# A first DFT step with d on the partitions, and two DMA transposes inside SBUF in place of an exchange through DRAM

## The chip, the cores and the metric

One core of one Trainium2 chip. The metric is the device time of one launch in microseconds; runs of one kernel mostly agree within 0.3%. A single core has no second die to compare with; every run used here is of the state "fast", within 1.5% of the fastest of its kernel. TensorE (PE) does the matrix multiplications and leaves the results in PSUM; ScalarE (ACT) and VectorE (DVE) bring them to SBUF, the memory that the next step reads (an "evacuation"). GpSimd (POOL) issues the loads of x and, at the start, of some weights; SyncE (SP) issues all other transfers. Sixteen DMA engines serve both queues: q1 is what SP issues, q0 what POOL issues.

## The reference

A Fourier layer, then a feed-forward block on its rows. Cut to what matters:

```python
X = np.fft.rfft(x, axis=1)                 # x: (8, 3008, 256)
Yr = Xr @ w_r - Xi @ w_i + b_r             # mix over the 256 features, real part
Yi = Xr @ w_i + Xi @ w_r + b_i
# soft threshold by 0.01 on Yr and Yi
y = np.fft.irfft(Yr + 1j * Yi, n=3008, axis=1)
h = y.reshape(24064, 256) @ w_in           # w_in: (256, 2048)
out = (s * np.maximum(h, 0) ** 2 + b) @ w_out
```

The kernel splits 3008 = 94 x 32: a DFT over n1 (94) with 96 real outputs, then one over n2 (32) with twiddles, the mix and the threshold, and the same two steps back. Batch by batch, the four steps are woven between the matmuls of the feed-forward block of an earlier batch.

## The kernel before

The first step of batches 1 to 7. `A_t` is the 94x96 DFT matrix. It is the stationary operand, and x streams past it:

```python
xpool = ctx.enter_context(tc.tile_pool(name="xp", bufs=4))      # one batch of x is 4 tiles
upool = ctx.enter_context(tc.tile_pool(name="up", bufs=3))
uspool = ctx.enter_context(tc.tile_pool(name="usp", bufs=5))
# ...
def s1_units(b, more_banks=False):
    ud = dpool.tile([96, N2, D], F16, name="ud", tag="ud")       # in DRAM
    hold = {}
    def unit(i):                                                 # 16 units
        c, j = divmod(2 * i, XCH)
        if j == 0:
            hold["u"] = upool.tile([P, XCH, D], F16, name="u", tag="u")
        ps = other_bank() if more_banks and i % 2 else one_bank()
        nc.tensor.matmul(ps[0:96, :], A_t[0:N1, :],
                         x16[(b, c)][0:N1, j * D : (j + 2) * D], start=True, stop=True)
        u = hold["u"]
        evac(u[0:96, j : j + 2, :], ps[0:96, :].rearrange("p (j d) -> p j d", j=2), 512)
        if j == XCH - 2:
            nc.sync.dma_start(out=ud[:, c * XCH : (c + 1) * XCH, :], in_=u[0:96])
        if i == N2 // 2 - 1:                                     # back, 128 rows (k, n) a tile
            uv = ud.rearrange("k n d -> (k n) d").rearrange("(q p) d -> p q d", p=P)
            for q in range(4):
                t = uspool.tile([P, 6, D], F16, name="us", tag="us")
                nc.sync.dma_start(out=t, in_=uv[:, 6 * q : 6 * q + 6, :])
                us[(b, q)] = t
```

The second step uses `us` as its stationary operand (`psf<-F_t,us` in the profile). The x loads and the schedule:

```python
def emit_load_x(b, first=None):            # first: a tile to wait for, used for batch 2 only
    for c in range(4):
        t = xpool.tile([P, XCH * D], F16, name="x16", tag="x16")
        if first is not None:
            gate = nc.gpsimd.tensor_copy(out=t[0:1, 0:1], in_=first)
        nc.gpsimd.dma_start(...)            # 94 rows of 4096 bytes, cast from f32
# ...
for b in range(2, B):
    s0, s1, s2 = mark[b - 2], mark[b - 1], mark[b]      # slots of the feed-forward block
    schedule(s0 + 40, s1 - s0 - 48, s1_units(b))
    schedule(s1 + 2, s2 - s1 - 30, s23_units(b))
    schedule(s2 - 14, 12, s4_units(b))
    if b + 1 < B:
        plan.setdefault(s1 + 6, []).append(lambda b=b: emit_load_x(b + 1))
```

A load of x for batch b+1 can start when the x tile of batch b in the same buffer has been read for the last time. What decides that is the order in which the first step reads its four x tiles.

## Time and profile before

| | before |
|---|---|
| time, median of 4 runs | 852.05 us |
| TensorE busy, of the span of 849.4 us | 835.0 us |
| one unit of the first step on TensorE (one matmul of 94x512) | 0.22 us |
| first-step exchange, per batch | 4 writes and 4 reads of 384 KB |
| end of the last evacuation of u to the first second-step matmul | 9.4 to 12.2 us |

TensorE is the bound and hardly ever waits; the exchange is hidden in that last row's window. The prediction shows the lines that say so. One more, of the page's DMA part:

```profile
HBM read 52.54 MB, written 46.66 MB: 117 GB/s over the span
```

### The profile page before, as it was taken

The page shows a single profiled execution, that of the slowest core. Times are in us where ns is not written, and L with a number is a line of the kernel's source. Part 1 is how long each engine was busy: PE and PEld are TensorE (multiplying, and loading weights), DVE is VectorE, ACT ScalarE, POOL GpSimd, SP SyncE. Part 2 cuts the span into 40 slices and gives each one's busy share as a digit, 9 for nine tenths or more (in the row PEclk, how much of TensorE's full clock was granted, in tenths as well). Part 3 has the DMA queues.
Part 4 walks back from the last instruction along what each step waited for, and adds up shares of the span by engine and source line. Part 5 has one row for each costly group of instructions (what it writes and reads, how often), then busy time and mean ns, then how long its engine had stood idle before and what let it go on. Part 6 is the DMA issues. An engine that isn't in the chain of part 4 may idle for free.

```text
span 849.4 us, 17085 instructions
## 1 busy us (share of the span) xinstructions
PE 835.0 (98%) x6645; PEld 600.5 (71%) x6645; DVE 697.0 (82%) x1027; ACT 643.2 (76%) x856; POOL 46.6 (5%) x72
## 2 busy tenths in 40 slices
PE   8899999999999999999999999999999999999997
PEld 7757777777677766777677776777667777766765
DVE  6898987888888987888878888888977888776674
ACT  5898887787778787787777887787877787766673
POOL 5321000000000000000000000000000000000000
PEclk9999999999999999999999999999999999999999
DMA  7937457324761367324662247613354223411111
GB/s 165 161 104 162 108 148 185 101 76 100 177 186 54 92 159 184 109 78 103 171 177 65 74 106 199 172 40 92 100 156 118 62 79 98 112 33 38 38 44 50
DMA packets 105458, 95.07 MB, mean 112 GB/s; under 512 B 9510, under 2 KB 97578, under 8 KB 104034
## 3 DMA queue, kind: packets, MB, share of 16 engines
q1 hardware_dynamic: 98930, 79.57, 32.6%
q0 software_dynamic: 6448, 14.42, 10.7%
q8 instruction: 52, 0.85, 0.4%
q14 instruction: 28, 0.23, 0.1%
HBM read 52.54 MB, written 46.66 MB: 117 GB/s over the span
## 4 chain that ended last, share of the span: by engine, by line
PE 88%; DVE 4%; ACT 3%; DMA 2%; issue 1%; POOL 0%; SPq 0%; DVEq 0%; ACTq 0%; POOLq 0%
PE psa L832 36%; PE psh L761 36%; PE psf L627 4%; PE psf L562 2%; PE psf L613 2%; PE psf L598 2%; PE psf L657 2%; PE psf L710 2%; ACT rt L768 1%; DVE gt L775 1%; DMA x<-in_x_dram 1%; DMA out_dram<-ost 1%; PE psh L410 1%; ACT yt L160 0%; ACT vs L160 0%
## 5 line engine op out<-in xcount | busy, mean ns | idle before, releaser
L768 ACT ACTIVATE rt<-psh 128x1024 f32<-128x1024 f32 (+2 forms) x384 | 387.1, 1009 | 119.1 <-PE psh L761 117.7
L775 DVE TENSOR_TENSOR gt<-rt 128x1024 f16<-128x1024 f32 (+2 forms) x321 | 384.0, 1199 | 98.1 <-ACT rt L768 97.4
L832 PE MATMUL psa<-w_out_t,gt 128*128 128x256 f16 (+1 forms) x3024 | 454.3, 272 | 0.1
L832 PEld LDWEIGHTS <-gt 128*128 128x128 f16 (+1 forms) x3024 | 300.9, 101 | 187.2 <-issue 1.7
L761 PE MATMUL psh<-yt,w_in 128*128 128x512 f16 (+1 forms) x1344 | 396.7, 378 | 0.3 <-ACT rt L768 0.3
L761 PEld LDWEIGHTS <-w_in 128*128 128x128 f16 x1536 | 142.9, 98 | 27.4 <-issue 2.1
L842 DVE SCALAR_TENSOR_TENSOR ost<-psa,s_bc,bias_bc 128x512 f32<-128x512 f32 (+2 forms) x97 | 71.0, 732 | 8.3 <-PE psa L832 7.1
L772 ACT ACTIVATE gt<-rt 128x1024 f16<-128x1024 f32 (+2 forms) x63 | 66.2, 1050 | 1.0
L632 DVE TENSOR_TENSOR ring<-psf,s 128x512 f16<-128x512 f32 x84 | 57.5, 684 | 3.7 <-PE psf L627 2.9
L160 ACT CAST v<-psf 128x512 f16<-128x512 f32 x78 | 45.3, 582 | 18.7 <-PE psf L657 18.7
L160 ACT CAST xf<-psf 128x512 f16<-128x512 f32 x82 | 47.9, 585 | 10.9 <-PE psf L598 10.8
L160 ACT CAST u<-psf 96x512 f16<-96x512 f32 x77 | 44.5, 580 | 11.0 <-PE psf L562 10.7
L761 PE MATMUL psh<-tail,w_in 128*128 128x512 f16 (+1 forms) x192 | 52.1, 353 | 0.0
L627 PE MATMUL psf<-W_g,xf 128*128 128x256 f16 x336 | 50.4, 273 | 0.0
L160 ACT CAST yt<-psf 128x480 f16<-128x480 f32 (+2 forms) x75 | 38.1, 520 | 13.6 <-PE psf L710 13.6
L189 POOL DMA_DIRECT2D x<-in_x_dram x36 | 18.9, 530 | 429.3 <-PE psf L562 428.0
L562 PE MATMUL psf<-x,A_t 94*96 94x512 f16 x104 | 39.7, 381 | 1.7 <-ACT yt L160 0.5
L638 DVE TENSOR_TENSOR ring<-ring,high 128x512 f16<-128x512 f16 x84 | 35.5, 423 | 2.3
L639 DVE TENSOR_TENSOR ring<-ring 128x512 f16<-128x512 f16 x84 | 35.5, 422 | 1.9
L637 DVE TENSOR_TENSOR ring<-ring,low 128x512 f16<-128x512 f16 x84 | 35.4, 421 | 1.6
L627 PEld LDWEIGHTS <-xf 128*128 128x128 f16 x336 | 32.9, 98 | 3.8
L710 PE MATMUL psf<-C_t,vs 96*128 96x96 f16 x448 | 33.0, 205 | 0.1
(89 smaller groups left out, 501.9 us busy)
## 6 DMA issues: line engine op xcount, KB each, us to landing
out_dram<-ost SPq DMA_DIRECT2D x152, 128.0 KB
ud<-u SPq DMA_DIRECT2D x28, 384.0 KB
us<-ud SPq DMA_DIRECT2D x28, 384.0 KB
vd<-v SPq DMA_DIRECT2D x42, 256.0 KB
vs<-vd SPq DMA_DIRECT2D x14, 768.0 KB
x<-in_x_dram POOLq DMA_DIRECT2D x28, 376.0 KB, 5.9
ring<-ring SPq DMA_DIRECT2D x280, 32.0 KB
out_dram<-ost SPq DMA_DIRECT2D x16, 120.0 KB
```

The source lines that it names most:

```text
L160: return None, nc.scalar.copy(out=dst, in_=src)
L562: nc.tensor.matmul(ps[0:96, :], A_t[0:N1, :], x16[(b, c)][0:N1, j * D : (j + 2) * D], start=True, stop=True,)
L627: nc.tensor.matmul(ps[:, r, :], xt[:, 2 - r, dc], W_g[:, dc, r], start=(dc == 0), stop=(dc == DC - 1),)
L632: nc.vector.tensor_tensor(out=t, in0=ps, in1=hold[i // 2][:, i % 2].unsqueeze(1).to_broadcast([P, 2, D]), op=ALU.add,)
L638: nc.vector.tensor_tensor(out=m, in0=m, in1=high, op=ALU.min)
L710: nc.tensor.matmul(ps[:, j * 96 : (j + 1) * 96], vs[(b, h)][:, k, ec * P : (ec + 1) * P], C_t, start=True, stop=True,)
L761: nc.tensor.matmul(o, w_in_t[dc][:, mc * P : (mc + 1) * P], r, start=(dc == 0), stop=(dc == DC - 1),)
L768: nc.scalar.activation(out=rt[:, :, 0:w], in_=ps[:, :, 0:w], func=AF.Relu)
L772: nc.scalar.activation(out=gt[:, :, 0:w], in_=rt[:, :, 0:w], func=AF.Square)
L775: nc.vector.tensor_tensor(out=gt[:, :, 0:w], in0=rt[:, :, 0:w], in1=rt[:, :, 0:w], op=ALU.mult)
L832: nc.tensor.matmul(ps[0:size, h, :], gts[(ti, mc // 2)][:, mc % 2, sub * size : (sub + 1) * size], w_out_t[:, mc, :], start=(mc == 0), sto ...
L842: nc.vector.scalar_tensor_tensor(out=ost[0:size, 0:k], in0=ps[0:size, 0:k], scalar=s_bc[0:size], in1=bias_bc[0:size, 0:k], op0=ALU.mult, o ...
```

## The change

The intent: batches 1 to 7 take the form that batch 0 has already. x becomes the stationary operand and `A_t` streams, so the result has d on all 128 partitions. The second step needs (k, n) on the partitions, and two DMA transposes per batch bring it there without DRAM. The buffers are resized to make room (not shown: `vs` goes from two buffers of half the rows to one of all rows, and constants of batch 0 share a tile). The core of the diff:

```diff
-    upool = ctx.enter_context(tc.tile_pool(name="up", bufs=3))
-    uspool = ctx.enter_context(tc.tile_pool(name="usp", bufs=5))
+    upool = ctx.enter_context(tc.tile_pool(name="up", bufs=1))
+    uspool = ctx.enter_context(tc.tile_pool(name="usp", bufs=1))
...
         def unit(i):
-            c, j = divmod(2 * i, XCH)
-            if j == 0:
-                hold["u"] = upool.tile([P, XCH, D], F16, name="u", tag="u")
+            dc, g = divmod(i, N2 // 4)
+            if i == 0:
+                hold["u"] = upool.tile([P, DC, 96, N2], F16, name="u", tag="u")
+                us[b] = uspool.tile([P, NPAIR, D], F16, name="us", tag="us")
+            c, h = divmod(g, 2)
             ps = other_bank() if more_banks and i % 2 else one_bank()
-            nc.tensor.matmul(
-                ps[0:96, :], A_t[0:N1, :], x16[(b, c)][0:N1, j * D : (j + 2) * D],
-                start=True, stop=True,
-            )
+            for j in range(4):
+                lo = (4 * h + j) * D + dc * P
+                nc.tensor.matmul(
+                    ps[:, j * 96 : j * 96 + 96], x16[(b, c)][0:N1, lo : lo + P],
+                    A_t[0:N1, :], start=True, stop=True,
+                )
             u = hold["u"]
-            evac(u[0:96, j : j + 2, :], ps[0:96, :].rearrange("p (j d) -> p j d", j=2), 512)
-            if j == XCH - 2:
+            evac(
+                u[:, dc, :, 4 * g : 4 * g + 4],
+                ps[:, 0:384].rearrange("p (n k) -> p k n", k=96), 384,
+            )
+            if g == N2 // 4 - 1:
                 nc.sync.dma_start(
-                    out=ud[:, c * XCH : (c + 1) * XCH, :], in_=u[0:96]
+                    out=us[b][:, :, dc * P : (dc + 1) * P],
+                    in_=u[:, dc].rearrange("p k n -> p (k n)"),
+                    transpose=True,
                 )
-            if i == N2 // 2 - 1: ...            # the four reads from DRAM: gone
...
-        emit_load_x(2, us[(1, 3)][0:1, 0, 0:1])
+        emit_load_x(2, us[1][0:1, 0, 0:1])
```

`dc, g = divmod(i, N2 // 4)` walks through all four x tiles for the first half of d, then once more for the second half.

More of the change, by code (lines that the diff above doesn't have):

```diff
@@ L144 @@
     vpool = ctx.enter_context(tc.tile_pool(name="vp", bufs=3))
-    vspool = ctx.enter_context(tc.tile_pool(name="vsp", bufs=2))
+    vspool = ctx.enter_context(tc.tile_pool(name="vsp", bufs=1))
     ypool = ctx.enter_context(tc.tile_pool(name="yp", bufs=2))
@@ L220 @@
             nc.sync.dma_start(out=b_g[r : r + 1, i], in_=bv.unsqueeze(0))
-    F_c = uspool.tile([P, NPAIR, 2, N2], F16, name="F_c", tag="us")
+    first_c = uspool.tile([P, 4, NPAIR * 64], F16, name="first_c", tag="us")
+    F_c = first_c[:, 0].rearrange("p (q r k) -> p q r k", q=NPAIR, r=2)
+    T_c = first_c[:, 1].rearrange("p (q k) -> p q k", q=NPAIR)
+    F_2 = [first_c[:, 2 + i].rearrange("p (q k) -> p q k", q=H) for i in range(2)]
     b_h = cpool.tile([P, D], F16, name="b_h")
@@ L227 @@
     sel_t = cpool.tile([P, P], F16, name="sel_t")
-    T_c = uspool.tile([P, NPAIR, 64], F16, name="T_c", tag="us")
     eye_t = cpool.tile([P, P], F16, name="eye_t")
@@ L275 @@
     nc.vector.memset(T_t, 0.0)
-    F_2 = [uspool.tile([P, H, P], F16, name="F_2", tag="us") for _ in range(2)]
     for f in F_2:
@@ L466, in inv_dft @@
             )
-        for h in range(2):
-            vs[(0, h)] = vspool.tile([96, HW, D], F16, name="vs", tag="vs")
+        vs[0] = vspool.tile([P, N2, D], F16, name="vs", tag="vs")
         def turn(ec, k):
@@ L477, in turn @@
                 )
-            h, n = divmod(8 * k, HW)
             evac(
-                vs[(0, h)][:, n : n + 8, ec * P : (ec + 1) * P],
+                vs[0][0:96, 8 * k : 8 * k + 8, ec * P : (ec + 1) * P],
                 ps[0:96].rearrange("p h (j e) -> p (h j) e", e=P), 1024,
@@ L489, in last_dft @@
             for j in range(8):
-                h, k = divmod(n2 + j, HW)
                 nc.tensor.matmul(
                     ps[j // 4][:, (j % 4) * 96 : (j % 4) * 96 + 96],
-                    vs[(0, h)][:, k, ec * P : (ec + 1) * P], C_t,
+                    vs[0][0:96, n2 + j, ec * P : (ec + 1) * P], C_t,
                     start=True, stop=True,
@@ L552, in s1_units @@
     def s1_units(b, more_banks=False):
-        ud = dpool.tile([96, N2, D], F16, name="ud", tag="ud")
         hold = {}
         def unit(i):
-            c, j = divmod(2 * i, XCH)
-            if j == 0:
-                hold["u"] = upool.tile([P, XCH, D], F16, name="u", tag="u")
-            ps = other_bank() if more_banks and i % 2 else one_bank()
-            nc.tensor.matmul(
-                ps[0:96, :], A_t[0:N1, :], x16[(b, c)][0:N1, j * D : (j + 2) * D],
-                start=True, stop=True,
-            )
-            u = hold["u"]
-            evac(u[0:96, j : j + 2, :], ps[0:96, :].rearrange("p (j d) -> p j d", j=2), 512)
-            if j == XCH - 2:
+            dc, g = divmod(i, N2 // 4)
[3 more added lines that the diff above has]
+            c, h = divmod(g, 2)
+            ps = other_bank() if more_banks and i % 2 else one_bank()
+            for j in range(4):
[4 more added lines that the diff above has]
+                )
+            u = hold["u"]
+            evac(
+                u[:, dc, :, 4 * g : 4 * g + 4],
+                ps[:, 0:384].rearrange("p (n k) -> p k n", k=96), 384,
+            )
+            if g == N2 // 4 - 1:
                 nc.sync.dma_start(
-                    out=ud[:, c * XCH : (c + 1) * XCH, :], in_=u[0:96]
-                )
-            if i == N2 // 2 - 1:
-                uv = ud.rearrange("k n d -> (k n) d").rearrange("(q p) d -> p q d", p=P)
-                for q in range(4):
-                    t = uspool.tile([P, 6, D], F16, name="us", tag="us")
-                    nc.sync.dma_start(out=t, in_=uv[:, 6 * q : 6 * q + 6, :])
-                    us[(b, q)] = t
+                    out=us[b][:, :, dc * P : (dc + 1) * P],
+                    in_=u[:, dc].rearrange("p k n -> p (k n)"),
+                    transpose=True,
+                )
         return [lambda i=i: unit(i) for i in range(N2 // 2)]
@@ L593, in fwd_unit @@
             ps = bank.rearrange("p (r c j k) -> p r c j k", r=2, c=DC, j=2)
-            t = us[(b, i // 3)]
             for j in range(2):
-                q = (2 * i + j) % 6
                 for dc in range(DC):
                     nc.tensor.matmul(
-                        ps[:, :, dc, j, :], t[:, q, dc * P : (dc + 1) * P],
+                        ps[:, :, dc, j, :], us[b][:, 2 * i + j, dc * P : (dc + 1) * P],
                         F_t[:, 2 * i + j, :], start=True, stop=True,
@@ L670, in inv_unit @@
                 vv = vd.rearrange("q (k n) e -> (q k) (n e)", n=N2)
+                t = vs[b] = vspool.tile([P, N2, D], F16, name="vs", tag="vs")
                 for h in range(2):
-                    t = vspool.tile([96, HW, D], F16, name="vs", tag="vs")
                     nc.sync.dma_start(
-                        out=t.rearrange("k n e -> k (n e)"),
+                        out=t[0:96, h * HW : h * HW + HW].rearrange("k n e -> k (n e)"),
                         in_=vv[:, h * HW * D : (h + 1) * HW * D],
                     )
-                    vs[(b, h)] = t
         units = []
@@ L708, in unit @@
             for j in range(w):
-                h, k = divmod(n2 + j, HW)
                 nc.tensor.matmul(
                     ps[:, j * 96 : (j + 1) * 96],
-                    vs[(b, h)][:, k, ec * P : (ec + 1) * P], C_t,
+                    vs[b][0:96, n2 + j, ec * P : (ec + 1) * P], C_t,
                     start=True, stop=True,
```

## The prediction

> **What bounds the kernel now.** I read the page first (busy time and the forty slices), then the chain of waits, then the table of groups, then stretches of the timeline in order of time around the step that changes, for the tensor engine and for the SP queue.
>
> ```profile
> span 849.4 us, 17085 instructions
> PE 835.0 (98%) x6645; PEld 600.5 (71%) x6645; DVE 697.0 (82%) x1027; ACT 643.2 (76%) x856; POOL 46.6 (5%) x72
> PE   8899999999999999999999999999999999999997
> DMA  7937457324761367324662247613354223411111
> ...
> PE 88%; DVE 4%; ACT 3%; DMA 2%; issue 1%; POOL 0%; SPq 0%; DVEq 0%; ACTq 0%; POOLq 0%
> ```
>
> The reader should see that TensorE is busy in every slice but the first two and the last, and that the chain that ended last is 88% TensorE. The DMA engines average well under half. A change pays here only if it shortens TensorE's stream, and it costs if it makes that stream wait. By windows, of the 794 us from 51 to 845 TensorE is busy 791.91.
>
> The groups that the change touches (columns: busy us, mean ns of one, idle before and its releaser):
>
> ```profile
> L160 ACT CAST u<-psf 96x512 f16<-96x512 f32 x77 | 44.5, 580 | 11.0 <-PE psf L562 10.7
> L562 PE MATMUL psf<-x,A_t 94*96 94x512 f16 x104 | 39.7, 381 | 1.7 <-ACT yt L160 0.5 <-DVE v L164 0.5 <-ACT u L160 0.3
> L710 PE MATMUL psf<-C_t,vs 96*128 96x96 f16 x448 | 33.0, 205 | 0.1
> L164 DVE CAST u<-psf 96x512 f16<-96x512 f32 x27 | 18.4, 682 | 6.1 <-PE psf L562 6.0
> L562 PEld LDWEIGHTS <-A_t 94*96 94x96 f16 x112 | 13.7, 123 | 3.0 <-issue 0.8
> ...
> L164 DVE CAST ut<-psf 128x384 f16<-128x384 f32 x8 | 4.5, 558 | 5.5 <-PE psf L361 5.4
> ...
> L160 ACT CAST ut<-psh 128x384 f16<-128x384 f32 x8 | 3.8, 479 | 7.8 <-PE psh L361 7.7
> ```
>
> The mean of a matmul contains its pipeline latency, so it is not what one costs in a full stream. For that I take start to start from the timeline. Columns: start, length, engine, line, operation, count.
>
> ```profile
> 209.33 0.38 PE L562 MATMUL psf<-x,A_t 94*96 94x512 f16 x1
> 209.55 0.59 PE L761 MATMUL psh<-yt,w_in 128*128 128x512 f16 x2
> ...
> 436.93 0.59 PE L710 MATMUL psf<-C_t,vs 96*128 96x96 f16 x10
> 437.36 0.60 PE L761 MATMUL psh<-tail,w_in 128*128 128x512 f16 x2
> ```
>
> One 94x512 matmul of today's first step holds the stream for 0.22 us (209.33 to 209.55). Ten matmuls with 96 moving columns and a new 128-column stationary operand each hold it for 0.43 us, or 43 ns each (436.93 to 437.36). The same 43 to 44 ns comes out for batch 0, which already computes its first step in the form that the change gives to the others (eight matmuls from 5.39 to 5.74 us).
>
> The SP queue at batch 5, where the last piece of the first step goes out and the rows come back:
>
> ```profile
> 435.31 0.31 SPq L569 DMA_DIRECT2D ud<-u  x1
> 437.91 0.60 SPq L794 DMA_DIRECT2D out_dram<-ost  x1
> 440.29 2.55 SPq L576 DMA_DIRECT2D us<-ud  x4
> ...
> 446.88 0.39 PE L598 MATMUL psf<-F_t,us 128*128 128x128 f16 x4
> ```
>
> The last write is issued at 435.3, the reads at 440.3 once it has landed, and the first consumer runs at 446.9. Over batches 1 to 7 I find 9.4, 12.2, 11.4, 10.8, 11.6, 10.4 and 11.6 us from the end of the last evacuation of u to the first matmul on us. That matmul waits for nothing in the trace: the exchange through DRAM is hidden completely. This window is what a transpose has to fit into.
>
> **What the Trainium skill says.** "TensorE: Matmul & The Clock Gate", section "Weight-path perf modes", says that the fast weight load is on when there are 128 weight columns. The trace agrees: loads of A_t (96 columns) take 123 ns, loads of vs (128 columns) 97 ns. After the change x is the stationary operand with 128 columns, so it is on the fast side. "DMA: Bandwidth & Descriptors", section "Latency and other measured facts", gives 261 GB/s measured for a DMA transpose with a non-contiguous middle dimension and 350 to 400 for a contiguous one; its section "Anatomy of one DMA" puts the fixed cost near 2 us. "VectorE: DVE Perf Modes", section "The three transpose paths", lists 1309 ns for one 128x128 transpose by DMA. The kernel before has no DMA transpose, so its trace neither confirms nor denies these two.
>
> **The change, part by part.**
>
> Matmuls. 7 batches x 16 = 112 matmuls of 94x512 become 448 of 94x96. One unit (an evacuated bank) goes from 0.22 us to 4 x 43 = 172 ns, which saves 48 ns. In plain terms, 94x512 writes only 96 of 128 output partitions, while the new form fills all 128. Ten units of batch 1 run before 51 us, where TensorE is waiting on evacuations anyway (its spacing there averages 388 ns), so I count 102 units: 102 x 0.048 = 4.9 us off the stream that sets the end. This is nearly the whole gain.
>
> Evacuations. Still 112, now 128x384 with 4-element pieces on the output side, as batch 0 does it: 479 instead of 580 ns on ScalarE, 558 instead of 682 on VectorE. The built program has 89 on ScalarE (80 before) and 23 on VectorE (32 before). ScalarE: 80 x 0.58 - 89 x 0.48 = 3.7 us less. VectorE: 32 x 0.68 - 23 x 0.56 = 8.9 us less. The balancing also moves a few other evacuations: ScalarE takes one more 128x1024 square and five fewer xf copies. All of it lies beside TensorE, whose recorded waits on these two engines add up to about 7 us, most of them before 51 us; I book 0 to 1 us.
>
> Transfers. Removed: 28 writes and 28 reads of 384 KB on the SP queue, 22 MB through DRAM out of 95. Added: 14 transposes of 768 KB (128 x 3072 x 2 bytes) inside SBUF, two per batch, the first at half of the first step and the second at its end. Estimate from the DMA page: 786 KB / 261 GB/s = 3.0 us, plus 2 us fixed, so about 5 us; with an output store and an x load on the same engines, 6 to 8 us. That fits the 9.4 to 12.2 us window, so I book no stall. The transposes free the DMA engines, but they bound nothing.
>
> Buffers. us, u and vs get one buffer each where there were five, three and two smaller ones. The first transpose of batch b+1 must wait until the second step of batch b has read us. At batch 4 to 5 the last such read starts at 393.3 and the half of the next first step is reached at 408.8; the other batches leave 11 to 22 us. That wait is free. x tiles are now released in the second half of the step instead of evenly, which bunches the next x loads near the second transpose; but they are needed some 50 us later. The gate that held back the x load of batch 2 until the last read of us now opens on the first transpose, so this load (four times 376 KB) can run beside batch 1's second transpose. Batch 1 also has the shortest window, so I book 0.6 us for it.
>
> Sum: 852.3 - 4.9 + 0.6 = 848.0 us.
>
> **The rivals.**
>
> A: the transpose becomes a new wait. It is one transfer with one completion, and the first second-step matmul needs all of it; before, the first quarter of the rows was enough. Against it: the skill's rate. For it: the 1309 ns entry, if 24 blocks of 128x128 simply went one after another, is 31 us, 20 us past the window. That would stall TensorE seven times, some 140 us, to about 990. In between, 14 us per transpose means 3 us x 7 = 20 us, about 868. The sign would be TensorE idle before the second-step matmuls, each batch, with the transpose as releaser.
>
> B: the transpose holds the SP queue or the DMA rings. At batch 5 the last two v writes were issued at 412.0 and 415.6 and the v reads at 418.3; they landed at 426 and are first used at 429.5, 3.4 us later. The first transpose goes out at about 409 just ahead of these. If it keeps the queue for under 6 us nothing moves. If it takes over 12 us, the inverse part is late too, by a few us per batch: 855 to 870.
>
> C: the smaller matmuls do not reach 43 ns, because each 96 columns now need a weight load of their own, where 512 shared one. At 55 ns (the 128-column spacing) a unit is 0.22 us and the gain is nil: 852. Against it: two places of this very trace show 43 to 44 with the same shape, one with the same x operand.
>
> D: relief of ScalarE and VectorE helps more than booked. Their waits on TensorE show that TensorE leads, so at most 2 us: 845.
>
> **Range and chances.** Below 844 would need gains that no view shows, as 102 units cannot give more than 4.9 us. I hold 65% for no stall worth naming (845 to 849), 22% for stalls of 1 to 2 us per batch or a rate between A's extremes (850 to 866), 12% for over 869. So 848, with 844 to 862 as the range. Faster by over 2% needs 835, below what TensorE's stream allows: 0.01. Slower by over 2% needs 869, that is a transpose of over 14 us: 0.12. The rest, 0.87, is within 2%.
>
> **What would show each step.** Matmuls: first-step groups of four with 172 ns start to start, and TensorE's busy time down by about 5 us. Evacuations: about 480 and 560 ns. Transfers: the second transpose landing 5 to 8 us after issue, no idle time of TensorE at the second step, SP held for less than 6 us. Buffers: the first transpose never waiting for TensorE's second-step reads. The prediction is wrong if a transpose takes over 12 us from issue to landing, if SP is held by it so long that stores or v writes pile up behind it, or if 94x96 matmuls with x stationary are spaced over 50 ns.

## The result, and the profile after

Changed kernel: 859.61 us, median of 4 runs (858.52 to 860.82). Before, in the same rounds: 852.05 us (851.17 to 854.75). The ratio is 1.0084, with a 95% interval of 1.0057 to 1.0111. Ratios here are the mean time of one kernel's fast runs over that of the other's of the same rounds, so they are not quite the ratio of the medians quoted. The kernel is clearly slower, by some 7 us, where I had expected it 4 us faster.

The page of the changed kernel: span, busy time, slices of the span for TensorE, its clock and DMA, memory traffic, and the chain by engine and by line.

```profile
span 859.0 us, 17659 instructions
PE 833.9 (97%) x6981; PEld 608.6 (71%) x6981; DVE 694.0 (81%) x1025; ACT 638.9 (74%) x858; POOL 46.5 (5%) x72
PE   8899999999999999799989999999999999999997
PEclk9999999999999999899999999999999999999999
DMA  7862368122851359422682226813262132411111
HBM read 41.53 MB, written 35.65 MB: 90 GB/s over the span
PE 86%; DMA 7%; ACT 3%; DVE 2%; issue 1%; POOL 0%; SPq 0%; DVEq 0%; ACTq 0%; POOLq 0%
```

11 MB less was read from DRAM and 11 MB less written, as intended. TensorE's row, full before, has dents in the 17th slice and, smaller, in the 21st, and the clock row drops in the 17th as well. In the chain, DMA has risen from 2% to 7%. Who waited for whom, TensorE's rows alone (waited for; us in total, times, longest):

```profile
PE psf L597 <- DMA us<-u: 8.4, 3, 4.1
PE psf L707 <- DMA vs<-vd: 2.4, 1, 2.4
```

Three waits for a transpose (one at batch 1, two at batch 4) and one for the v rows of the way back make 10.8 us. Neither wait was there before. The new first step itself does what was hoped (timeline of TensorE: start, length, what, count):

```profile
216.09 0.34 PE L564 MATMUL psf<-A_t,x 94*128 94x96 f16 x4
216.27 0.60 PE L758 MATMUL psh<-yt,w_in 128*128 128x512 f16 x2
```

Four matmuls hold the stream for 0.18 us, where one of 94x512 held it for 0.22. The evacuations are cheaper as well, on ScalarE and VectorE (mean in ns after the busy time):

```profile
L160 ACT CAST u<-psf 128x384 f16<-128x384 f32 x85 | 40.8, 481 | 13.6 <-PE psf L564 12.8
L164 DVE CAST u<-psf 128x384 f16<-128x384 f32 x19 | 10.5, 554 | 4.5 <-PE psf L564 4.4
```

The waits sit in few places. The largest is batch 4's; here is the SP queue around it (start, how long SP was held, what, count), then TensorE:

```profile
313.67 0.79 SPq L672 DMA_DIRECT2D vs<-vd  x2
314.94 7.91 SPq L574 DMA_TRANSPOSE us<-u  x1
322.91 7.22 SPq L791 DMA_DIRECT2D out_dram<-ost  x4
332.06 15.85 SPq L574 DMA_TRANSPOSE us<-u  x1
```

```profile
342.52 0.60 PE L829 MATMUL psa<-w_out_t,gt 128*128 128x256 f16 x4
347.26 0.29 PE L597 MATMUL psf<-F_t,us 128*128 128x128 f16 x1 [4.14 <-DMA us<-u]
350.01 0.50 PE L597 MATMUL psf<-F_t,us 128*128 128x128 f16 x3 [2.46 <-DMA us<-u]
350.30 1.06 PE L758 MATMUL psh<-yt,w_in 128*128 128x512 f16 x2
```

The reader should see two things. The second transpose held SP for 15.85 us, and TensorE stood for 4.14 and 2.46 us because it landed so late. And the two 128x512 matmuls after it take 1.06 us where such a pair takes 0.60: the clock has been halved. The trace's clock record grants 0.5 for 6.8 us from 347.1, and for 3.4 us from 439.3, after the wait for v.

Elsewhere the transposes are quick: undisturbed ones hold SP for 3.6 to 3.8 us, and in the trace's packet records their last packet ends about 5.1 us after the issue (46.88 to 51.99 for batch 1's first). Batch 1's second one held SP for 9.38 us and ended 10.95 us after its issue; TensorE stood for 1.8 us. Batch 4's first one ended 24.8 us after its issue, and the second, queued behind it, 17.4 us after.

**The sum.** Profile against profile, 859.0 - 849.4 = 9.6 us. Waits: +10.8. Clock: of the 6.8 us at half clock TensorE stood for 2.46, so (6.8 - 2.46) / 2 = 2.2, and 3.4 / 2 = 1.7 for the second: +3.9. Matmuls: -4.9 (measured alone below). Together +9.8.

**Theories.** What makes some transposes late? In the packet records (one for each row that is moved), x rows of 4096 bytes on q0 are moving in each of the bad stretches. The x loads stand differently now: each x tile of batch b is read twice, and comes free only in the second half of the step. So the loads for batch b+1 bunch up there, where both transposes are (beside batch 4's first step POOL issued them at 305, 315, 323 and 332 us before, and at 318, 322, 327 and 332 after). Theory S: x loads starve the transposes. The main rival, H: a transpose is slow or held up in the SP queue by itself, behind the v reads that stand just ahead of batch 4's first one.

### The profile page after: what moved, and what is told of

It is laid out like the page before. It is cut to its first block, busy times and chain, and to the rows that moved or that the text cites. A ratio compares the mean times of both kernels' runs of the same rounds, so it can differ in the third digit from the quotient of the medians.

```text
span 859.0 us, 17659 instructions
## 1 busy us (share of the span) xinstructions
PE 833.9 (97%) x6981; PEld 608.6 (71%) x6981; DVE 694.0 (81%) x1025; ACT 638.9 (74%) x858; POOL 46.5 (5%) x72
## 4 chain that ended last, share of the span: by engine, by line
PE 86%; DMA 7%; ACT 3%; DVE 2%; issue 1%; POOL 0%; SPq 0%; DVEq 0%; ACTq 0%; POOLq 0%
PE psa L829 36%; PE psh L758 35%; PE psf L626 4%; DMA us<-u 3%; PE psf L597 2%; PE psf L612 2%; PE psf L656 2%; PE psf L564 2%; PE psf L707 2%; DMA vs<-vd 1%; DMA x<-in_x_dram 1%; ACT rt L765 1%; DMA ring<-ring 1%; DMA vd<-v 1%; PE psh L411 1%
## 5 line engine op out<-in xcount | busy, mean ns | idle before, releaser
L758 PEld LDWEIGHTS <-w_in 128*128 128x128 f16 x1536 | 138.0, 98 | 14.3 <-issue 0.5
L839 DVE SCALAR_TENSOR_TENSOR ost<-psa,s_bc,bias_bc 128x512 f32<-128x512 f32 (+2 forms) x97 | 71.1, 733 | 14.3 <-PE psa L829 10.5
L160 ACT CAST xf<-psf 128x512 f16<-128x512 f32 x77 | 45.0, 586 | 19.7 <-PE psf L597 19.7
L160 ACT CAST u<-psf 128x384 f16<-128x384 f32 x85 | 40.8, 481 | 13.6 <-PE psf L564 12.8
L160 ACT CAST yt<-psf 128x480 f16<-128x480 f32 (+2 forms) x68 | 34.9, 532 | 13.7 <-PE psf L707 13.5
L597 PE MATMUL psf<-F_t,us 128*128 128x128 f16 x336 | 33.3, 221 | 8.4 <-DMA us<-u 8.4
L564 PEld LDWEIGHTS <-x 94*128 94x128 f16 x448 | 30.8, 98 | 7.2 <-issue 3.4
```

The costliest lines, as they stand in the source:

```text
L160: return None, nc.scalar.copy(out=dst, in_=src)
L564: nc.tensor.matmul(ps[:, j * 96 : j * 96 + 96], x16[(b, c)][0:N1, lo : lo + P], A_t[0:N1, :], start=True, stop=True,)
L597: nc.tensor.matmul(ps[:, :, dc, j, :], us[b][:, 2 * i + j, dc * P : (dc + 1) * P], F_t[:, 2 * i + j, :], start=True, stop=True,)
L758: nc.tensor.matmul(o, w_in_t[dc][:, mc * P : (mc + 1) * P], r, start=(dc == 0), stop=(dc == DC - 1),)
L839: nc.vector.scalar_tensor_tensor(out=ost[0:size, 0:k], in0=ps[0:size, 0:k], scalar=s_bc[0:size], in1=bias_bc[0:size, 0:k], op0=ALU.mult, o ...
```

## The experiments

Ten kernels ran, with the kernel before.

**1. One gate moved.** The x load of batch 2 waits for the second transpose of batch 1, not the first.

```diff
-        emit_load_x(2, us[1][0:1, 0, 0:1])
+        emit_load_x(2, us[1][0:1, 0, P : P + 1])
```

> Changed kernel, with one edit: the gate that holds back the x load of batch 2 reads the half of us that the second transpose of batch 1 writes, not the first half. Theory S (the transposes are starved: x loads on the other DMA queue share each engine packet by packet, 4096 bytes against 256): batch 1's second transpose lands about 3 to 4 us after issue instead of 11, its stall of 1.9 us at the second step goes, batches 4 and 5 are as before: about 857.5 us, 2 us under the changed kernel. Rival H (the transpose is slow or held up by the SP queue by itself, x loads do not matter): still 9 us on SP, no change, 859.6.

Measured: 858.99 us (855.99 to 860.16), ratio 1.0083 (1.0064 to 1.0102). The SP queue at batch 1, in the changed kernel and in this one:

```profile
56.10 9.38 SPq L574 DMA_TRANSPOSE us<-u  x1
56.73 3.60 SPq L574 DMA_TRANSPOSE us<-u  x1
```

3.60 us instead of 9.38, and batch 1's stall is gone from the profile; batch 4's is there unchanged (3.9 and 2.6 us). The cause in batch 1, x loads beside the transpose, is thereby shown. As a time it is inconclusive: the change of 1.8 us is within the spread of these runs, which is wider than usual. This profile doesn't have the wait for v either; one profile of each kernel can't say how often it comes.

**2. All x loads gated.** From batch 2 on they wait for the second transpose of the batch before.

```diff
-        emit_load_x(2, us[1][0:1, 0, 0:1])
+        emit_load_x(2, us[1][0:1, 0, P : P + 1])
...
-            plan.setdefault(s1 + 6, []).append(lambda b=b: emit_load_x(b + 1))
+            plan.setdefault(s1 + 6, []).append(
+                lambda b=b: emit_load_x(b + 1, us[b][0:1, 0, P : P + 1])
+            )
```

> Changed kernel, with every x load from batch 2 on held until the second transpose of the batch before has landed. Theory S: all second transposes are held on SP for under 4.5 us and land in under 6; no idle TensorE before the second step; the late v rows of batch 5 (2.5 us) are gone too if x loads delayed them; total 847 to 848.5 us, faster than both kernels. Rival H: the stalls of batches 4 (7 us) and 5 remain, 856 or more. Rival L (x loads now come too late or collide with the small moves of the second step): new waits on x or ring, 850 to 860.

Measured: 846.97 us (846.72 to 848.23), ratio 0.9952 (0.9938 to 0.9966); correct. Span and busy time from its page, then the SP queue around batch 4's first step:

```profile
span 845.1 us, 17702 instructions
PE 830.1 (98%) x6981; PEld 606.7 (72%) x6981; DVE 694.1 (82%) x1025; ACT 638.6 (76%) x858; POOL 53.1 (6%) x92
```

```profile
312.37 0.79 SPq L672 DMA_DIRECT2D vs<-vd  x2
313.69 8.75 SPq L574 DMA_TRANSPOSE us<-u  x1
322.49 2.66 SPq L791 DMA_DIRECT2D out_dram<-ost  x4
330.79 4.28 SPq L574 DMA_TRANSPOSE us<-u  x1
```

The v reads still stand ahead of the first transpose and hold it up (8.75 us), yet the second is held for 4.28 us instead of 15.85, and TensorE no longer waits for us or vs. So the v reads alone do not make the second one late; H falls, and S predicted the time. This kernel beats both. They may still help: in the changed kernel the first row of batch 4's first transpose moved at 320.6, 5.7 us after the issue, where 1.2 to 1.3 us is usual, and so it met the x loads, which no other first transpose did. No run takes the v reads away and leaves the x loads.

**3 and 4. The matmul term alone.** Without the transposes, so the result is wrong. The first attempt zeroed us once with VectorE.

```diff
-                us[b] = uspool.tile([P, NPAIR, D], F16, name="us", tag="us")
+                if 1 not in us:
+                    us[1] = uspool.tile([P, NPAIR, D], F16, name="us", tag="us")
+                    nc.vector.memset(us[1], 0.0)
+                us[b] = us[1]
...
-            if g == N2 // 4 - 1:
+            if False:
```

> Changed kernel without the transposes; us is set to zero once, so the result is wrong on purpose. Everything else, the bunched x loads too, stays. The matmul term alone: 4.9 us under before, so 847 to 848 us, if the transposes cause all stalls. If the bunched x loads delay the v rows of batch 5 by themselves, that stall (2.5 us, and about 1.7 us at the half clock that follows) stays and the time is about 851 us. If the matmul term is not there, 852 or more without any stall.

Measured: 851.27 us, ratio 1.0001 (0.9987 to 1.0014). This was my mistake, not a finding: the zeroing falls into the start, where it took VectorE 2.6 us from 44.7 us on and TensorE then ran at half clock for 6.8 us; the first feed-forward matmul came at 55.5 us instead of 49.1. After that the profile has no stall. The second attempt adds nothing at the start; the second step reads w_out in place of us:

```diff
-                us[b] = uspool.tile([P, NPAIR, D], F16, name="us", tag="us")
+                us[b] = w_out_t
...
-                        ps[:, :, dc, j, :], us[b][:, 2 * i + j, dc * P : (dc + 1) * P],
+                        ps[:, :, dc, j, :], us[b][:, (2 * i + j) % MC, dc * P : (dc + 1) * P],
```

> Changed kernel without the transposes; the second step reads w_out instead of us, so the result is wrong on purpose, and nothing is added at the start (the zeroing did that in the run before). The matmul term alone: 4.9 us under before, 846 to 848 us, and about the same as with all x loads gated. If the gain of the gated kernel came from the gates and not from the matmuls, this one stays at 851 to 852.

Measured: 847.16 us (846.65 to 847.70), ratio 0.9942 (0.9927 to 0.9957), against 852.07 for before: 4.9 us. That is the matmul term as predicted (with what the evacuations may add), and experiment 2 has all of it within the noise.

**5. The gates on the kernel before.** Its x loads from batch 3 on wait for the last read of us.

```diff
-            plan.setdefault(s1 + 6, []).append(lambda b=b: emit_load_x(b + 1))
+            plan.setdefault(s1 + 6, []).append(
+                lambda b=b: emit_load_x(b + 1, us[(b, 3)][0:1, 0, 0:1])
+            )
```

> The kernel before with the same gates: the x loads of batch 3 on wait for the last read of us of the batch before. If the gates themselves are worth nothing without the transposes: 851 to 852.5 us, no change. If they are what made the gated kernel fast: 847.

Measured: 853.98 us (851.72 to 855.39), ratio 1.0020 (1.0002 to 1.0037), with no wait for us in the profile. The gates are worth nothing by themselves; they only keep what the matmuls gain. In its profile the first feed-forward matmul comes at 51.7 us instead of 49.6, before any gate is reached, so the 2 us that it is slower are not theirs.

**6. Another way to the same end.** The halves of d inside, the x tiles outside, so x tiles come free evenly as before and both transposes go out at the end.

```diff
-            dc, g = divmod(i, N2 // 4)
+            g, dc = divmod(i, DC)
```

> Changed kernel with the two d halves inside and the chunks of x outside, so x tiles come free evenly again (after units 3, 7, 11 and 15) and both transposes go out together at the end of the step. Theory S: batch 4 loses its pile-up of first transpose and x loads; but the two transposes take about 3.7 us each on SP one after the other beside one x load, so they land 8 to 11 us after the last unit, at the edge of the window of 9.4 to 12.2 us. Batch 1 keeps its stall of 2 to 4 us, the rest 0 to 2 us each: 849 to 854 us. If the order of the units did not matter: 859.

Measured: 847.46 us (847.10 to 847.95), ratio 0.9946 (0.9931 to 0.9961); correct, no stall. I expected 849 to 854 and was too gloomy. The first transpose is almost done with its 5 us when the second is issued, and only one x load was beside them: the second ended 5.1 to 9.1 us after its own issue. The margin is thin, though. At batch 4 it ended at 341.1, and the first matmul on it started at 342.0. The order of two loops decides here between 859.6 and 847.5 us.

**7. The dose turned up.** All four x loads of a batch are released together, at the last evacuation of u, so that they start with the second transpose.

```diff
+            last_u[b] = hold["u"][0:1, 1, 0, N2 - 1 : N2]
...
-        emit_load_x(2, us[1][0:1, 0, 0:1])
+        emit_load_x(2, last_u[1])
...
-            plan.setdefault(s1 + 6, []).append(lambda b=b: emit_load_x(b + 1))
+            plan.setdefault(s1 + 6, []).append(
+                lambda b=b: emit_load_x(b + 1, last_u[b])
+            )
```

> Changed kernel with the x loads of batch 2 on released, all four together, at the last evacuation of u, so that they start with the second transpose in every batch. Theory S: every second transpose is starved as batch 1's was, held on SP for 8 to 12 us and landing 10 to 12 us after issue; stalls of 0 to 3 us in most batches, 852 to 862 us in all. First transposes are clear of x loads. If x loads beside the transpose do not matter and only the pile-up with the v reads of batch 4 does: 847 to 849.

Measured: 854.37 us (853.75 to 854.93), ratio 1.0024 (1.0008 to 1.0041). The range held, the details only in part. Batch 3's second transpose ended 15.6 us after its issue (240.02 to 255.64) and stalled TensorE for 5.5 us; those of batches 2, 4, 5 and 6, with x loads beside them too, ended in 5.8 to 9.8 us, where 5.1 is the undisturbed time, and stalled it for 0.5 us in all. So loads released there delay the transpose every time, but whether they break the window varies.

**8. Smaller x rows.** Each x load cut in four, rows of 1024 bytes.

```diff
-            parts = 2 if b == 0 else 1
+            parts = 2 if b == 0 else 4
```

> Changed kernel, with each x load of batches 1 to 7 cut into four transfers of 1024-byte rows instead of 4096. Theory S, packet by packet: beside x loads the transpose's share grows about fourfold, so batch 4's second transpose is held on SP for some 6 to 9 us instead of 15.9 and its stall of 7 us mostly goes: 849 to 854 us. Rival B (plain bandwidth: x loads take a fixed share of the engines' bytes, whatever the packet): no change of batch 4, 858 to 861. Smaller rows can also make the x loads themselves slower.

Measured: 860.04 us (854.29 to 862.82), ratio 1.0092 (1.0057 to 1.0127). Half a miss. Batch 4's second transpose was held for 10.5 us instead of 15.9 and its stall fell from 6.6 to 5.0 us, as a larger share would do. But batch 1's stall rose to 4.1 us, and batches 2 and 3 got stalls of 0.8 and 1.0. In the packet records most 1024-byte x rows take 96 or 98 ns and most 4096-byte ones 322 or 324, so four small ones take 384 or more; the x loads are on the engines for longer. The time matches rival B; the transpose of batch 4 does not.

**9 and 10. Is it the transpose, or just small rows?** A plain copy of the same 768 KB in place of each transpose, result wrong; rows of 256 bytes (9) and of 6144 (10).

```diff
-                    in_=u[:, dc].rearrange("p k n -> p (k n)"),
-                    transpose=True,
+                    in_=u[:, dc].rearrange("p k n -> p (k n)").rearrange("p (q e) -> p q e", q=NPAIR),
```

```diff
-                    out=us[b][:, :, dc * P : (dc + 1) * P],
+                    out=us[b].rearrange("p q e -> p (q e)")[:, dc * 96 * N2 : (dc + 1) * 96 * N2],
                     in_=u[:, dc].rearrange("p k n -> p (k n)"),
-                    transpose=True,
```

> Changed kernel with each transpose replaced by a plain copy of the same 768 KB inside SBUF, in rows of 256 bytes (result wrong on purpose); x loads bunched as in the changed kernel. Theory P (small rows on the SP queue lose against 4096-byte x rows, transposing has no part in it): the second copies of batches 1 and 4 are late as the transposes were, stalls at the second step of 5 to 9 us in all, 855 to 861 us. Theory X (it is particular to the transpose): the copies land within 7 us of issue also beside x loads, no stall, 847 to 849 us.

> The same with the plain copy in rows of 6144 bytes. Theory P: large rows hold their own against x rows, landing in 5 to 8 us, no stall or under 1 us, 847 to 849 us. Theory X: the same, 847 to 849 us. If any SBUF transfer beside the x loads is late whatever its rows: 855 or more.

Measured: 851.77 us (850.78 to 851.90), ratio 1.0000 (0.9985 to 1.0015), for rows of 256 bytes; 846.92 us (846.49 to 849.12), ratio 0.9953 (0.9936 to 0.9969), for rows of 6144. Neither theory had the first number. TensorE's wait in 9:

```profile
PE psf L596 <- DMA us<-u: 2.9, 1, 2.9
```

One wait, of batch 1, with 3.4 us of half clock from 70.0 on: 2.9 + 1.7 - 4.9 = -0.3 us, which is the time measured. So batch 1's stall needs no transpose: a plain copy in rows of 256 bytes beside four x loads is enough.

That 10 has no stall does not show that the size of the rows decides. Alone, its copy ends 3.3 us after its issue, where the transpose and the copy of 9 take 5.1. So its first copy lands sooner and opens the gate sooner: the x loads of batch 2 go out at 51.5 to 55.4 us, not at 55.2 to 58.3 as in 9. Even so batch 1's second copy ended 9.0 us after its issue, at 65.3, just before TensorE used it at 65.8. Over its own time alone it lost 5.7 us beside the x loads, the transpose 5.8 and the copy of 9 7.0. About half of that comes before the first row moves, 4.0 to 4.3 us after the issue in all three, where 1.2 to 1.4 is usual. What the size of the rows adds is not shown.

From 61 to 63 us of experiment 9, with both moving, the records have 95 x rows against 108 small ones, sixteen to one in bytes for each pair. The Trainium skill, "DMA: Bandwidth & Descriptors", section "Queues, rings and completion order", says that an engine takes turns between the queues and moves a packet of several descriptors at each turn. The counts of these 2 us would fit equal turns; but from 326 to 331 us of the same run 185 x rows stand against 1457 small ones, so one for one is no rule here.

But batch 4, the larger stall, is not there in 9, although the same x loads fall on the same place. Windows of the three kernels in which x rows and SBUF transfers move together: the changed kernel at batch 4, experiment 9 at batch 4, experiment 7 at batch 3. The columns are the stretch, its length, busy us and count of PE, PEld, DVE, ACT and POOL, the granted clock, the busy share of the DMA engines, and GB/s.

```profile
323.00:333.00 10.00, 9.74 (x104) 7.15 (x102) 8.22 (x10) 7.27 (x12) 1.03 (x2) 1.00 1.01 62
```

```profile
326.00:331.00 5.00, 4.84 (x50) 3.42 (x49) 4.45 (x5) 3.60 (x6) 0.51 (x1) 1.00 1.16 226
```

```profile
243.00:254.00 11.00, 8.91 (x78) 6.42 (x76) 8.65 (x9) 6.44 (x9) 0.93 (x1) 1.00 1.19 68
```

In all three the engines are shown fully busy. With a plain copy they move 226 GB/s; with a transpose under way 62 and 68, x rows and transpose together (26 in experiment 7 from 246 to 253 us, once x rows are moving). A transpose alone moved 217 GB/s from 49 to 51 us in the changed kernel, and 275 from 347 to 349. So there are two effects: beside a bunch of x loads each of these three transfers comes later, by 5.7 to 7.0 us at batch 1, and with a transpose in flight together with x rows both can drop to under a third. Why the second happens, no run here shows. It does not always happen (from 60 to 63 us in the changed kernel 132 x rows and 172 rows of batch 1's transpose moved together at 195 GB/s). That stays open.

## Why the prediction was right or wrong

The class, "within 2%", and the range, 844 to 862, held. The point, 848, was 11.6 us low, and the sign was wrong: I had 4 us of gain, and it was a loss of 7.6. That the range held is in part luck. Its branch of 850 to 866 us stood for 1 to 2 us of stall in each batch, or for a slower transpose; the loss came from two batches, one late v read and half clock. The prediction's own sign of being wrong, over 12 us from issue to landing, did come (24.8 and 17.4 us at batch 4), and so did SP held for over 6 us (6.4 to 15.85 us, four times).

- **Matmuls: right.** 172 ns a unit predicted, 0.18 us measured, and 4.9 us for the whole term predicted and measured (experiment 4). The loads of x as the stationary operand took 98 ns, the fast side, as expected. Rival C falls.
- **Evacuations: right.** 479 and 558 ns predicted, 481 and 554 measured, with no visible effect on the end. Rival D falls.
- **The transpose by itself: right.** About 5 us predicted, 5.1 measured; the reading of 31 us in rival A falls. The 2 us of fixed cost in that sum is given by the skill's page for transfers that GpSimd issues, and SP issued these, so that the sum fits so well is not proof of its parts.
- **The step that failed** is in the paragraph on transfers: "with an output store and an x load on the same engines, 6 to 8 us. That fits the 9.4 to 12.2 us window, so I book no stall." With one x load beside it the second transpose did take 6.9 to 8.0 us and fitted (batches 2, 3, 5 and 6). Wrong was the overlap that it took for granted, one x load: at batch 1 all four ran beside the second transpose, which took 10.95 us, and at batch 4 they ran beside both, which took 24.8 and 17.4. The stalls, with the one for v, cost 10.8 us plus 3.9 us of half clock.
- **The buffers paragraph saw the cause and asked the wrong question of it.** It says that x loads would be bunched near the second transpose, "but they are needed some 50 us later". True, but it is the transpose that is late, not x. For batch 1 it booked 0.6 us where the stall was 1.8. And batch 4, whose first step is the shortest (34 us in the kernel before, 48 to 51 for the other batches from 2 on), it did not single out.
- **Rivals A and B: right in kind, wrong in cause.** A's sign, TensorE idle before the second step with the transpose as releaser, appeared at 3 waits in 2 batches, not in every one. B's late v rows appeared once (2.4 us), in batch 4's way back, which runs beside batch 5's first step; the prediction and two expectations call it batch 5's. The last v write was issued at 424.00 and the reads at 430.68; with all x loads gated, 413.70 and 417.49. In the changed kernel an x load was issued just before that last write, at 423.67, so x loads are the likely cause here too, but a run without this wait (experiment 1) has nearly the same gap, so this is argued and not shown.
- **Half clock: not in the prediction at all.** It added 3.9 us to the 9.0 us of stalls that set it off (6.6 in batch 4's second step, 2.4 at the v rows).

## What to carry to other kernels

When a change reorders the reads of a buffer, look at what the buffer's release sets off, and what it will then run beside; a load that has ample time can still take the engines from a transfer that has none. A transfer with a short window, a DMA transpose above all, should not meet several bulk loads on another queue: gate the loads on the transfer's landing, or order the loops so that loads start elsewhere. Before undoing a change that came out slower, measure its terms apart: here the gain was there in full, and one loop order or one gate brought it out, 847 us against 852.

## What the Trainium skill lacked or had wrong

- "DMA: Bandwidth & Descriptors", sections "Latency and other measured facts" and "Rules for kernel authors": a rate for a transpose (261 GB/s; here, alone, 217 and 275 GB/s in two stretches of 2 us), and that a transpose next to ordinary DMAs needs nothing. The page means that as a matter of correctness, and it held; for speed it does not: beside loads of x on the other queue, 62 and 68 GB/s for both together, and up to 24.8 us from issue to the last packet instead of 5.1.
- The same page has no time measured on this chip for how long a transpose holds the queue that issues it (it has cycle counts of other generations only): 3.6 to 3.8 us for 128 x 3072 two-byte elements undisturbed, 15.85 at worst; a plain copy of the same bytes held it for 0.5 to 0.7.
- "VectorE: DVE Perf Modes", section "The three transpose paths": 1309 ns for one 128x128 block by DMA must not be multiplied; 24 blocks in one transfer took 5.1 us.
- "TensorE: Matmul & The Clock Gate", section "Why this matters for your kernels": no gaps over about 3 us. Here a wait of 2.35 us (437.1 to 439.45) already brought 3.4 us at half clock, granted from 439.3 on; one of 1.8 us at batch 1 did not.
